# Linear attention with a two-layer MLP in one core's program: the first tile laid out anew

## The chip, the cores and the metric

The kernel runs on one core of a Trainium2 chip. The metric is the device time of one execution in microseconds. Five engines take part: TensorE (PE in the profile; PEld is its loading of weights), VectorE (DVE), ScalarE (ACT), GpSimd (POOL) and SyncE (SP), which here issues every DMA. Each works through its own list of instructions in order, and semaphores hold an instruction until what it needs is there.

## The reference, cut to what matters

```python
def _attn_ref(q, k, v, omega):           # q, k, v: (8, 8, 576, 64); omega: (128, 64)
    def phi(x):
        h = einsum('bhsd,md->bhsm', x, omega) - sum(x * x) / 2
        return exp(h - max(h)) / sqrt(m)
    q_p, k_p = phi(q * scale), phi(k * scale)
    kv, z = einsum('bhsm,bhsd->bhmd', k_p, v), sum(k_p, axis=2)
    return einsum('bhsm,bhmd->bhsd', q_p, kv) / (einsum('bhsm,bhm->bhs', q_p, z) + 1e-6)
def _moe_ref(x, g_ln, w_ch1, w_ch2):     # x: (8, 576, 512), the heads side by side
    xn = (x - mean(x)) / sqrt(var(x) + 1e-6) * g_ln
    return x + maximum(xn @ w_ch1, 0) @ w_ch2          # w_ch1: 512x2048, w_ch2: 2048x512
```

## The kernel before, in words

**Tiles.** The 8 x 576 rows of x make 36 blocks of 128 rows; four blocks make a tile of 512 rows, and there are nine tiles. The MLP of a tile runs over f = 0 to 15, blocks of 128 hidden columns: `mm1(t, f)` (L684) multiplies the transposed x - mu of the tile with the f-th 128 columns of W1, 12 matmuls into one bank; `relu` (L705) writes the result in a high and a low part (ACT L709, DVE L711); `mm2(t, f)` (L720) multiplies that with the f-th 128 rows of W2, 12 matmuls into four banks that stay open over all f; `result` (L740) adds x at f = 15 and stores. Each product is made of three fp32r matmuls of high and low parts. PE's order is mm1(0), mm1(1), mm2(0), mm1(2), mm2(1) and so on.

**Weights.** The host hands W1 and W2 over as 64-bit numbers, 32 blocks of 128 rows by 512 columns (512 KB each). `gen_w` (L347) loads a block, puts each number together from its two halves (a sign or mask step, L361 on ACT or L369 on DVE; a scaling, L242 or L244; two steps of DVE, L363 or L373, then L377), multiplies W1 by g (L242 or L244, "g" the layer norm's gain, one number per partition) and takes the low part (L388 for W1, L394 for W2). A block of W1 holds 128 rows of W1 and 512 columns, so the mm1 of f = 0 to 3 take one column strip out of each of the blocks 0 to 3, and all four have to be there ahead of mm1(0); likewise 4 to 7 ahead of mm1(4).

**Attention.** A key block (`gen_k`, L418): a projection on PE (L481), its negated maximum on DVE (L484), exponentials on ACT (L490, eight of them in two halves), and the *sums* (L453), 16 small matmuls that add k_p times v into a pair of banks. For the first batch the five key blocks add up in banks 6 and 7, and ACT copies them out once (L470, `kv`). A query block (`gen_q`, L498): a projection (L513), a copy to SBUF (L236 is the copy helper's line on ACT), a maximum over partitions on POOL (L543), the subtraction on DVE (L548) and the exponential on ACT (L551). Then the *products* (`gen_x`, L574): 16 small matmuls (L590), 1 / denominator and x on DVE (L598, L600, L602), statistics (L619, L621). `gen_xnT` (L648) subtracts mu on DVE (L658), PE transposes (L671), ACT and DVE write the high and the low part (L675, L677). The first tile needs five key blocks, four query blocks and four products ahead of its first mm1; all later ones are done between the matmuls of the MLP, "visits" to a pair of banks.

**Idle matmuls.** Until the MLP starts, `warm` (L319) issues matmuls of a constant on itself (128x252 bf16, the tile named spin, L322) into the unused columns of bank 7. `gen_warm` fills what the layout sees as free time of PE with them, and sums and products have one after every second head inside them (L457, L594).

**What sets the order.** `Plan` (L67) is a planner that runs while the program is built. Each step of a generator names the engine and what the step costs there (`yield dve(n)`, `yield "run", {ACT: 0.66, DVE: 0.45}`); the planner keeps a clock for each engine, takes the step that can start first, by rank among equals, and emits it. So the costs decide only the order of instructions on each engine, on which engine a step with two prices runs, and how many idle matmuls stand between others. A step seen from another engine is ready HOP = 0.2 us after its end.

Of the kernel before, what the change touches and what calls it, by code (L numbers as in the profile page):

```python
# [41 lines left out]
class Part:  # L42


    def __init__(self, rank, order, gen, after):
        self.rank, self.order = rank, order
        self.holds = 0
        self.gen = gen
        self.after = after
        self.eng, self.end = None, 0.0  # L50
        self.want = None
# [6 lines left out]
    def seen(self):  # L58

        return max(self.after, self.end + Plan.HOP)  # L60

    def ready(self, eng):
        t = max(self.after, self.end + (Plan.SAME.get(eng, 0.0) if eng == self.eng else Plan.HOP))
# [3 lines left out]
class Plan:  # L67
# [10 lines left out]
    HOP = 0.2  # L78
    SAME = {ACT: 0.16, DVE: 0.13, POOL: 0.1}
    SLACK = 0.4  # L80
# [79 lines left out]
    def starts(self, part, queue):  # L160

        times = ((max(part.ready(e), self.free_at[e]), e, cost) for e, cost in part.want[1].items())
        return min(times, key=lambda t: t[0] + t[2] + queue[t[1]])

    def run(self):
        while self.ready:
# [18 lines left out]
            part.eng = eng  # L185
            if eng == SP:
# [10 lines left out]
def favor_ffn(ctx, tc, kT, kTr, vF, vR, qT, qD, omT, gT, w1, w2, out):  # L197
# [24 lines left out]
    def act(n, k=1, c=0.17):  # L222
        return "run", {ACT: k * (c + 0.00083 * n)}

    def dve(n, k=1, c=0.157):
        return "run", {DVE: k * (c + 0.00104 * n)}
# [97 lines left out]
    def gen_const():  # L324
# [6 lines left out]
        nc.sync.dma_start(g_sb, gT)  # L331
        done(("g",))
# [14 lines left out]
    def gen_w(n, f):  # L347
# [9 lines left out]
        eng = yield "run", {ACT: 0.66, DVE: 0.45}  # L357
        t = tile_of(wt, [P, DM], U32)
        sign = 0x80000000
        if eng == ACT:  # L360
            nc.scalar.activation(out=t, in_=r[:, :, 0], func=AF.Copy, scale=2.0**-29 * 7.49 / 8)  # L361
            yield dve(DM)
# [3 lines left out]
            eng = yield "run", {ACT: 0.66, DVE: 0.45}  # L366
            scaled(eng, f32(r[:, :, 1]), f32(r[:, :, 1]), 2.0**-112)
        else:
            nc.vector.tensor_scalar(out=t, in0=r[:, :, 1], scalar1=sign, scalar2=None, op0=ALU.bitwise_and)  # L369
            eng = yield "run", {ACT: 0.66, DVE: 0.45}  # L370
            scaled(eng, f32(r[:, :, 1]), f32(r[:, :, 1]), 2.0**-112)
            yield dve(DM)
# [3 lines left out]
        yield dve(DM)  # L376
# [5 lines left out]
        eng = yield "run", {ACT: 0.66, DVE: 0.45}  # L382
        w = wparts[n, f] = tile_of(tag, [P, 2, DM], F32R)
        if n == 1:
            g = g_sb[:, f % NK : f % NK + 1]
            scaled(eng, w[:, 0], f32(t), g)
            yield dve(DM)
# [3 lines left out]
        else:  # L391
            copy(eng, w[:, 0], f32(t))
            yield dve(DM)
# [24 lines left out]
    def gen_k(b, c, r, kraw, v, early, t_v, n_kp):  # L418
# [20 lines left out]
        def sums():  # L439
# [9 lines left out]
            yield us(PE, VISIT + 0.94 if mlp_on else 1.4)  # L449
            pv = two(t_b, 4 * (D + 1)).rearrange("p s (a b) -> p s a b", b=D + 1)  # L450
            for h in range(H):
# [5 lines left out]
                warm(h % 2)  # L457
# [10 lines left out]
            else:  # L468
                eng = yield "run", {ACT: 0.6, DVE: 0.7}
# [6 lines left out]
        yield us(PE, VISIT + 0.9)  # L476
# [10 lines left out]
        for s in range(2):  # L487
            yield act(M, 4)
# [9 lines left out]
    def gen_q(c):  # L498
# [3 lines left out]
        if c < QF:  # L502
# [6 lines left out]
            yield us(PE, VISIT + 0.88)  # L509
# [5 lines left out]
        else:  # L515
# [20 lines left out]
        eng = yield "run", {ACT: 1.02} if first else {ACT: 1.02, DVE: 1.23}  # L536
# [5 lines left out]
        yield us(POOL, 3.7)  # L542
# [4 lines left out]
        yield dve(8 * P)  # L547
        nc.vector.tensor_tensor(out=qc, in0=qc, in1=mx, op=ALU.subtract)  # L548
        free(t_m, mx_turn)
        yield act(8 * P)  # L550
# [23 lines left out]
    def gen_x(c, b_turn):  # L574
# [23 lines left out]
        nc.vector.tensor_scalar(out=dn, in0=pn[:, :, :, D], scalar1=EPS * M, scalar2=None, op0=ALU.add)  # L598
        yield us(DVE, 0.18)
# [249 lines left out]
```

## Time and profile before

| | us |
|---|---|
| median of 3 runs (lowest, highest) | 1027.58 (1027.01, 1027.80) |
| the profiled execution, its time | 1027.65 |
| the profiled execution, its span | 1025.9 |
| first matmul of mm1(0) starts | 57.54 |
| PE busy over the span | 1016.9 (99%) |
| DVE, ACT busy over the span | 474.9 (46%), 341.5 (33%) |

A row of a timeline reads: start, duration, engine, line, operation, output<-inputs with buffer numbers left out, shapes, count, and in brackets how long the engine had been idle and what ended that. The duration of one instruction is longer than the step to the next one's start, since they overlap by some 0.1 us on an engine. The chain view follows the end of a stretch back to what released it.

### The profile page before, as it was taken

Reading aid. Unit: us, or ns where it says so; the run is one execution under the profiler, and the core shown is the slowest. Engines: PE = TensorE matmul, PEld = TensorE weight load, DVE = VectorE, ACT = ScalarE, POOL = GpSimd, SP = SyncE. Lnnn points to the kernel's source line nnn. Section 1 sums busy time; section 2 is a strip of 40 time slices with the busy share of each in tenths; the row PEclk is TensorE's granted clock in tenths of the full one; section 3 lists DMA queues with packets and bytes.
Section 4 is the critical chain, followed back from the end, with each engine's and each line's share of the span. In section 5 each row is a group of like instructions: output and inputs, shape, how many; then the busy total and the mean of one; then the engine's idle time right before and its main releaser. Section 6 shows DMA issues by size and latency. Waiting matters only on the chain.

```text
span 1025.9 us, 16419 instructions
## 1 busy us (share of the span) xinstructions
PE 1016.9 (99%) x7033; PEld 817.5 (80%) x7033; DVE 474.9 (46%) x772; ACT 341.5 (33%) x700; POOL 118.9 (12%) x44
## 2 busy tenths in 40 slices
PE   9999999999999999999999999999999999999998
PEld 6787778788778777887788778878887888888886
DVE  6698887355375242663238422651364133113112
ACT  6387735334254243343213421231133111111100
POOL 4001040121121021031003100130022000000000
PEclk9999999999999999999999999999999999999999
DMA  9226423112122120320013100200020010001001
GB/s 355 111 82 216 156 73 129 47 61 71 43 87 88 37 63 21 104 94 22 1 62 105 51 1 1 103 21 1 9 95 21 1 42 1 1 1 42 1 1 41
DMA packets 26344, 63.13 MB, mean 62 GB/s; under 512 B 3104, under 2 KB 4256, under 8 KB 26272
## 3 DMA queue, kind: packets, MB, share of 16 engines
q1 hardware_dynamic: 26272, 62.09, 17.5%
q8 instruction: 55, 0.90, 0.4%
q14 instruction: 17, 0.14, 0.0%
HBM read 52.64 MB, written 9.44 MB: 61 GB/s over the span
## 4 chain that ended last, share of the span: by engine, by line
PE 96%; DVE 3%; ACT 1%; issue 1%
PE b L698 14%; PE b L731 13%; PE b L699 12%; PE b L700 12%; PE b L733 12%; PE b L732 12%; PE b L453 4%; PE b L481 4%; PE b L590 4%; PE b L322 3%; PE b L671 2%; PE b L531 1%; PE b L532 1%; PE b L513 1%; DVE quad L525 1%
## 5 line engine op out<-in xcount | busy, mean ns | idle before, releaser
L711 DVE SCALAR_TENSOR_TENSOR hid<-b,hid 128x512 fp32r<-128x512 f32 x144 | 99.5, 691 | 365.7 <-ACT hid L709 365.0
L709 ACT ACTIVATE hid<-b 128x512 fp32r<-128x512 f32 x144 | 86.3, 599 | 445.7 <-PE b L700 445.5
L698 PE MATMUL b<-xnT,w 128*128 128x512 f32 x576 | 231.1, 401 | 0.0
L731 PE MATMUL b<-w,hid 128*128 128x512 f32 x576 | 231.1, 401 | 0.0
L699 PE MATMUL b<-xnT,w 128*128 128x512 f32 x576 | 224.8, 390 | 0.0
L732 PE MATMUL b<-w,hid 128*128 128x512 f32 x576 | 224.6, 390 | 0.0
L733 PE MATMUL b<-w,hid 128*128 128x512 f32 x576 | 224.6, 390 | 0.0
L700 PE MATMUL b<-xnT,w 128*128 128x512 f32 x576 | 224.4, 390 | 0.0
L543 POOL PARTITION_ALL_REDUCE quad<-quad x34 | 111.1, 3281 | 661.4 <-ACT quad L236 537.7
L698 PEld LDWEIGHTS b<-xnT,w 128*128 128x128 f32 x576 | 108.1, 188 | 28.9 <-issue 4.1
L731 PEld LDWEIGHTS b<-w,hid 128*128 128x128 f32 x576 | 108.1, 188 | 24.4 <-issue 0.2
L733 PEld LDWEIGHTS b<-w,hid 128*128 128x128 f32 x576 | 108.1, 188 | 23.2
L700 PEld LDWEIGHTS b<-xnT,w 128*128 128x128 f32 x576 | 108.1, 188 | 23.2
L732 PEld LDWEIGHTS b<-w,hid 128*128 128x128 f32 x576 | 108.3, 188 | 20.5
L699 PEld LDWEIGHTS b<-xnT,w 128*128 128x128 f32 x576 | 108.2, 188 | 20.6
L490 ACT ACTIVATE kp<-b,mb 128x128 f32<-128x128 f32 (+1 forms) x296 | 81.2, 382 | 44.6 <-DVE mb L484 44.4
L484 DVE TENSOR_REDUCE mb<-b 128x8 f32<-128x1024 f32 (+1 forms) x40 | 48.8, 1220 | 35.3 <-PE b L481 35.3
L548 DVE TENSOR_TENSOR quad<-quad,quad 128x1024 f32<-128x1024 f32 x34 | 49.5, 1454 | 16.6 <-POOL quad L543 16.5
L236 ACT COPY quad<-b 128x1024 f32<-128x1024 f32 x36 | 36.6, 1018 | 59.0 <-PE b L532 44.2
L551 ACT ACTIVATE quad<-quad 128x1024 f32<-128x1024 f32 x36 | 38.3, 1065 | 42.5 <-DVE quad L548 42.5
L590 PEld LDWEIGHTS b<-kv,quad 128*64 128x64 f32 x1152 | 37.6, 137 | 15.4 <-issue 8.5
L525 DVE TENSOR_TENSOR quad<-quad,quad 64x1024 fp32r<-64x1024 f32 x28 | 38.7, 1383 | 21.5 <-ACT quad L523 20.9
(73 smaller groups left out, 770.2 us busy)
## 6 DMA issues: line engine op xcount, KB each, us to landing
w<-w SPq DMA_DIRECT2D x32, 512.0 KB, 7.2
quad<-qD SPq DMA_DIRECT2D x28, 512.0 KB, 3.3
out<-x SPq DMA_DIRECT2D x36, 256.0 KB, 2.0
v<-vF SPq DMA_DIRECT2D x28, 260.0 KB, 3.0
wide<-kT SPq DMA_DIRECT2D x28, 256.0 KB, 3.5
wide<-qT SPq DMA_DIRECT2D x8, 256.0 KB, 3.3
w<-vF SPq DMA_DIRECT2D x4, 260.0 KB, 4.4
v<-vR SPq DMA_DIRECT2D x8, 130.0 KB, 2.6
```

Source lines behind the costliest of these rows:

```text
L490: nc.scalar.activation(out=kp[0:r, j], in_=pk[0:r, s, j % 4], func=AF.Exp, scale=1.0, bias=mb[0:r, j : j + 1])
L543: nc.gpsimd.partition_all_reduce(mx.rearrange("p a b -> p (a b)"), qc.rearrange("p a b -> p (a b)"), P, bass_isa.ReduceOp.max)
L548: nc.vector.tensor_tensor(out=qc, in0=qc, in1=mx, op=ALU.subtract)
L590: nc.tensor.matmul(pn[a : a + D, h // 4, h % 4], phi[:, h % 2, h // 2, a : a + D], kvs[b][1][:, h], start=True, stop=True,)
L698: nc.tensor.matmul(ph, w[:, 0, cs], xnT[:, 0, k], start=(k == 0), stop=False)
L699: nc.tensor.matmul(ph, w[:, 1, cs], xnT[:, 0, k], start=False, stop=False)
L700: nc.tensor.matmul(ph, w[:, 0, cs], xnT[:, 1, k], start=False, stop=(k == NK - 1))
L709: nc.scalar.activation(out=hl[:, 0], in_=ph, func=AF.Relu)
L711: nc.vector.scalar_tensor_tensor(out=hl[:, 1], in0=ph, scalar=0.0, in1=f32(hl[:, 0]), op0=ALU.max, op1=ALU.subtract)
L731: nc.tensor.matmul(accs[i], hl[:, 0, cs], w[:, 0], start=(f == 0), stop=False)
L732: nc.tensor.matmul(accs[i], hl[:, 0, cs], w[:, 1], start=False, stop=False)
L733: nc.tensor.matmul(accs[i], hl[:, 1, cs], w[:, 0], start=False, stop=(f == NF - 1))
```

## The change

It does six things.

1. Sums and products have no idle matmul inside them (both calls `warm(h % 2)` go). Their cost in the plan before the MLP goes from 1.4 to 0.37 + 0.94 us. `gen_warm` stays as it is.
2. W1's blocks 0 to 3 hold other numbers: the host packs, for f = 0 to 3, all 512 rows of the 128 columns of f into block f, four row strips side by side. So mm1(f) takes all it needs from block f alone. A partition now holds four rows of W1, so g differs by strip: on ACT the multiplication is four instructions of 128 columns, on DVE one, and the low part is four instructions on DVE in place of one. Blocks 4 to 15 are as before.
3. The ranks of W1's blocks 0 to 3 in the plan go from f - 4 to 2f - 1 (each times 0.5), so block 3 ranks behind blocks 4 and 5.
4. mu - x is taken instead of x - mu, on ACT or on DVE (`either`), and g is negated once on DVE. The ACT form is new: AF.Identity with bias mu and scale -1. Of the 36, 20 go to ACT and 16 stay on DVE.
5. The costs in the plan are others throughout, smaller by some 0.1 us for most steps; what another engine sees costs 0.13 to 0.2 us by engine (LAT) in place of HOP; a DVE step marked "two" costs 1.0 us more (LOCK) where POOL is busy.
6. The copy of a projection to SBUF may go to DVE for the first tile too (`{ACT: 0.91, DVE: 1.13}`).

Counted over the whole program the idle matmuls go from 217 to 118; all other matmuls are the same in number and shape. The projections, sums and products ahead of mm1(0) are the same five, five and four.

```diff
     def starts(self, part, queue):
...
+            if e == DVE and part.want[-1] == "two" and start < self.free_at[POOL]:
+                cost += Plan.LOCK
...
-        eng = yield "run", {ACT: 0.66, DVE: 0.45}
+        if n == 1 and f < NK:
+            eng = yield either(0.92, 0.6)
+            w = wparts[n, f] = tile_of(tag, [P, 2, DM], F32R)
+            if eng == ACT:
+                for k in range(NK):
+                    cs = slice(k * P, (k + 1) * P)
+                    scaled(eng, w[:, 0, cs], f32(t[:, cs]), g_sb[:, k : k + 1])
+            else:
+                nc.vector.tensor_tensor(
...
+            yield "run", {DVE: 0.84}, "two"
+            for k in range(NK):
+                cs = slice(k * P, (k + 1) * P)
+                nc.vector.scalar_tensor_tensor(
+                    out=w[:, 1, cs], in0=f32(t[:, cs]), scalar=g_sb[:, k : k + 1], in1=f32(w[:, 0, cs]),
+                    op0=ALU.mult, op1=ALU.subtract,
+                )
...
+            return
+        eng = yield either(0.58, 0.34)
...
-            yield us(PE, VISIT + 0.94 if mlp_on else 1.4)
+            yield "run", {PE: VISIT + 0.94}, 0.03
...
-                warm(h % 2)
...
-        eng = yield "run", {ACT: 1.02} if first else {ACT: 1.02, DVE: 1.23}
+        eng = yield "run", {ACT: 0.91, DVE: 1.13}
         copy(eng, qc, pq)
...
-        yield us(PE, VISIT + 0.94 if mlp_on else 1.4)
+        yield "run", {PE: VISIT + 0.94}, 0.03
...
-            warm(h % 2)
...
-            yield us(DVE, 0.5)
-            nc.vector.tensor_scalar(out=xn, in0=x, scalar1=mu, scalar2=None, op0=ALU.subtract)
+            eng = yield either(0.58, 0.4)
+            if eng == ACT:
+                nc.scalar.activation(out=xn, in_=x, func=AF.Identity, bias=mu, scale=-1.0)
+            else:
+                nc.vector.tensor_scalar(out=xn, in0=x, scalar1=mu, scalar2=-1.0, op0=ALU.subtract, op1=ALU.mult)
...
-            yield wait("w", 1, f // NK * NK + k)
+            yield wait("w", 1, f if f < NK else f // NK * NK + k)
...
-            cs = slice(f % NK * P, (f % NK + 1) * P)
+            w = wparts[1, f if f < NK else f // NK * NK + k]
+            cs = slice((k if f < NK else f % NK) * P, ((k if f < NK else f % NK) + 1) * P)
...
-        plan.add(RW + RS * (2 * f - 7 if f >= NK else f - NK), gen_w(1, f))
+        plan.add(RW + RS * (2 * f - 7 if f >= NK else 2 * f - 1), gen_w(1, f))
```

Three places show what the new plan makes of the order.

PE, from the first to the second of the first tile's four products, before (quad_158 and quad_185 are the exponentials of the first and second query block, kv_86 the summed keys, spin the idle matmul's operand):

```order
L590 MATMUL b<-kv_86,quad_158 64x65 x4
L322 LDWEIGHTS spin
L322 MATMUL b<-spin 128x252
L590 MATMUL b<-kv_86,quad_185 64x65 x4
L322 LDWEIGHTS spin
```

And in the changed program, all four products (quad_156, quad_187, quad_213, quad_290):

```order
L627 MATMUL b<-kv_86,quad_156 64x65 x16
L627 MATMUL b<-kv_86,quad_187 64x65 x16
L627 MATMUL b<-kv_86,quad_213 64x65 x16
L336 LDWEIGHTS spin
L336 MATMUL b<-spin 128x252
L627 MATMUL b<-kv_86,quad_290 64x65 x16
```

Before, an idle matmul stands behind every fourth small matmul of this list (and one or two between visits); now one stands between the third and the fourth product.

DVE, from the first query block's subtraction to the maximum of the fourth key block (mb_240), before:

```order
L548 TENSOR_TENSOR quad_158<-quad_158,quad_174 128x1024
L436 MEMSET w_120_94 128x8
L369 TENSOR_SCALAR wide_264<-w_00_153 128x512
L369 TENSOR_SCALAR wide_268<-w_10_160 128x512
L244 TENSOR_SCALAR w_00_153<-w_00_153 128x512
L244 TENSOR_SCALAR w_10_160<-w_10_160 128x512
L484 TENSOR_REDUCE mb_240<-b 128x8
L548 TENSOR_TENSOR quad_185<-quad_185,quad_218 128x1024
```

And the same stretch in the changed program (there the maximum is mb_234):

```order
L585 TENSOR_TENSOR quad_156<-quad_156,quad_176 128x1024
L474 MEMSET w_120_94 128x8
L385 TENSOR_SCALAR wide_264<-w_00_151 128x512
L585 TENSOR_TENSOR quad_187<-quad_187,quad_206 128x1024
L521 TENSOR_REDUCE mb_234<-b 128x8
```

Four steps on weights went from ahead of this maximum, one of them is left, and the second query block's subtraction came ahead of it.

SP, the loads behind those of keys and queries (w1_00 is block 0 of W1, w2_10 block 1 of W2, and so on), before:

```order
L352 DMA w1_00_153<-w1 128x1024
L352 DMA w1_10_160<-w1 128x1024
L352 DMA w1_20_162<-w1 128x1024
L505 DMA wide1_157<-qT 128x512
L352 DMA w2_00_181<-w2 128x1024
L352 DMA w2_10_188<-w2 128x1024
L352 DMA w1_30_444<-w1 128x1024
L352 DMA w1_40_461<-w1 128x1024
L352 DMA w1_50_546<-w1 128x1024
L352 DMA w2_20_573<-w2 128x1024
```

And in the changed program:

```order
L368 DMA w1_00_151<-w1 128x1024
L368 DMA w2_00_158<-w2 128x1024
L368 DMA w1_10_161<-w1 128x1024
L542 DMA wide1_155<-qT 128x512
L368 DMA w2_10_178<-w2 128x1024
L368 DMA w1_20_189<-w1 128x1024
L368 DMA w1_40_473<-w1 128x1024
L368 DMA w1_50_495<-w1 128x1024
L368 DMA w2_20_608<-w2 128x1024
L368 DMA w1_30_677<-w1 128x1024
```

The first mm1 waited for blocks 0 to 3 of W1, the last of which was the sixth load of weights; it now waits for block 0, the first. Block 3 went from sixth to ninth, behind blocks 4 and 5.

More of the change, by code (lines that the diff above doesn't have):

```diff
@@ L58, in seen @@
     def seen(self):
-        return max(self.after, self.end + Plan.HOP)
+        return max(self.after, self.end + self.lat)
     def ready(self, eng):
-        t = max(self.after, self.end + (Plan.SAME.get(eng, 0.0) if eng == self.eng else Plan.HOP))
+        t = max(self.after, self.end + (Plan.SAME.get(eng, 0.0) if eng == self.eng else self.lat))
         return t + (Plan.SLACK if eng == PE != self.eng and 0 <= self.rank < Plan.FILL else 0.0)
 class Plan:
-    HOP = 0.2
-    SAME = {ACT: 0.16, DVE: 0.13, POOL: 0.1}
-    SLACK = 0.4
+    LAT = {PE: 0.2, ACT: 0.15, DVE: 0.13, POOL: 0.15, SP: 0.2}
+    SAME = {ACT: 0.2, DVE: 0.19, POOL: 0.1}
+    SLACK = 0.45
+    LOCK = 1.0
     FILL, IDLE = 10000, 20000
@@ L160, in starts @@
     def starts(self, part, queue):
-        times = ((max(part.ready(e), self.free_at[e]), e, cost) for e, cost in part.want[1].items())
+        times = []
+        for e, cost in part.want[1].items():
+            start = max(part.ready(e), self.free_at[e])
+            if e == DVE and part.want[-1] == "two" and start < self.free_at[POOL]:
+                cost += Plan.LOCK
+            times.append((start, e, cost))
         return min(times, key=lambda t: t[0] + t[2] + queue[t[1]])
@@ L185, in run @@
             part.eng = eng
+            part.lat = part.want[2] if len(part.want) > 2 and part.want[2] != "two" else Plan.LAT[eng]
             if eng == SP:
@@ L220, in f32, with act, dve, dve2 @@
         return ap.bitcast(F32)
[L222 to L226, printed above, removed]
+    def act(n, c=0.066):
+        return "run", {ACT: c + 0.00083 * n}
+    def dve(n, c=0.07):
+        return "run", {DVE: c + 0.00104 * n}
+    def dve2(n):
+        return "run", {DVE: 0.07 + 0.00104 * n}, "two"
+    def either(a, d):
+        return "run", {ACT: a, DVE: d}, "two"
     def us(eng, t):
@@ L331, in gen_const @@
         nc.sync.dma_start(g_sb, gT)
+        yield us(DVE, 0.08)
+        nc.vector.tensor_scalar(out=g_sb, in0=g_sb, scalar1=-1.0, scalar2=None, op0=ALU.mult)
         done(("g",))
@@ L365, in gen_w @@
             )
-            eng = yield "run", {ACT: 0.66, DVE: 0.45}
+            eng = yield either(0.58, 0.34)
             scaled(eng, f32(r[:, :, 1]), f32(r[:, :, 1]), 2.0**-112)
@@ L369, in gen_w @@
             nc.vector.tensor_scalar(out=t, in0=r[:, :, 1], scalar1=sign, scalar2=None, op0=ALU.bitwise_and)
-            eng = yield "run", {ACT: 0.66, DVE: 0.45}
+            eng = yield either(0.58, 0.34)
             scaled(eng, f32(r[:, :, 1]), f32(r[:, :, 1]), 2.0**-112)
-            yield dve(DM)
+            yield dve2(DM)
             nc.vector.scalar_tensor_tensor(
@@ L386, in gen_w @@
             scaled(eng, w[:, 0], f32(t), g)
-            yield dve(DM)
+            yield "run", {DVE: 0.66}, "two"
             nc.vector.scalar_tensor_tensor(
@@ L468, in sums @@
             else:
-                eng = yield "run", {ACT: 0.6, DVE: 0.7}
+                eng = yield "run", {ACT: 0.53, DVE: 0.61}
                 copy(eng, o, pv)
@@ L744, in result @@
         t_st, st = stats[t]
-        yield dve(DM)
+        yield us(DVE, 0.68)
         nc.vector.scalar_tensor_tensor(
```

59 lines of the change are left out of this document (33 added, 26 removed).

## The prediction

> **What bounds the kernel now.** I read the page first, then the stretches (busy time by window), then the chain of waits between 28 and 58 us, then the timelines of DVE, ACT and POOL there. From the page, the row of PE and the chain by engine:
>
> ```profile
> PE 1016.9 (99%) x7033; PEld 817.5 (80%) x7033; DVE 474.9 (46%) x772; ACT 341.5 (33%) x700; POOL 118.9 (12%) x44
> ...
> PE 96%; DVE 3%; ACT 1%; issue 1%
> ```
>
> Four stretches (length, busy time and instructions by engine, granted clock, DMA share, GB/s), cut at the end of the first batch's sums, at the first mm1 and at about the end of the first tile's MLP:
>
> ```profile
> 0.00:31.00 31.00, 29.28 (x335) 20.53 (x336) 21.57 (x29) 20.59 (x51) 14.24 (x12) 1.00 0.96 366
> 31.00:57.50 26.50, 24.78 (x282) 19.96 (x282) 18.34 (x43) 9.22 (x17) 0.00 (x0) 1.00 0.06 24
> 57.50:157.00 99.50, 99.50 (x696) 76.70 (x695) 87.85 (x151) 65.15 (x129) 14.17 (x4) 1.00 0.41 141
> 157.00:1022.00 865.00, 863.26 (x5725) 700.34 (x5723) 346.28 (x552) 246.53 (x506) 90.48 (x28) 1.00 0.13 42
> ```
>
> From 57.5 us on PE is the bound: it is busy all but 1.7 of 964.5 us, and the change leaves the number and shape of its matmuls there alone. So the time moves with the first 57.5 us, with waits that PE gets afterwards, and with nothing else. In the stretch 31 to 57.5 PE looks just as busy, yet the chain shows with what (start, length, what; x is the count of instructions):
>
> ```profile
> by line: PE b L322 62.6%; PE b L590 20.4%; PE b L671 5.8%; PE b L453 5.1%; DVE x L602 2.3%; ACT kv L236 2.0%; PE b L698 0.8%; issue 0.7%; DVE dn L598 0.6%
> ...
> 30.59 0.38 PE b L453 x8
> 30.97 0.98 PE b L322 x8
> 31.97 0.60 ACT kv L236
> 32.61 0.81 PE b L322 x6
> 33.42 0.38 PE b L590 x8
> 33.80 0.21 PE b L322
> ...
> 42.47 0.38 PE b L590 x8
> 42.86 0.77 PE b L322 x6
> 43.86 1.79 PE b L322 x15
> 45.67 0.70 DVE x L602
> 46.42 2.31 PE b L322 x20
> 48.73 0.44 PE b L671 x4
> ...
> 53.91 0.44 PE b L671 x4
> 54.34 3.44 PE b L322 x32
> 57.78 0.23 PE b L698
> ```
>
> L322 is the idle matmul: 62.6% of the way from 28 to 58 us. PE's list is in order, so idle matmuls that the layout put there too generously delay the real work behind them. They even hold DVE up, because they write to bank 7, from which the fourth product is read; two rows of DVE, the first waiting for an idle matmul:
>
> ```profile
> 43.65 0.17 DVE L598 TENSOR_SCALAR dn<-b 128x8 f32<-128x8 f32 x1 [2.36 <-PE b L322]
> 56.68 0.76 DVE L388 SCALAR_TENSOR_TENSOR w<-wide,g_sb,w 128x512 fp32r<-128x512 f32 x1
> ```
>
> The second row is the low part of W1's block 3, done at 57.44, 0.1 ahead of the first mm1: the second thing for which the MLP waits, and one that mm1(0) no longer needs.
>
> **The change, part by part.** I go from S, the end of the first batch's sums (30.97 now), to the first mm1 (57.54), then to what comes ahead of S, then to the first tile.
>
> *From S to mm1: 26.6 us now.* One price is needed, 16 small matmuls (32 passes) without idle ones inside. The MLP's visits show it:
>
> ```profile
> 139.43 1.08 PE b L590 x32
> ```
>
> I take 1.2 with the switch, where 33.42 to 42.86 shows 9.44 / 4 = 2.36 each now. An idle matmul takes 3.44 / 32 = 0.11, and 0.21 behind a small one.
>
> - S to first product: 2.45 now. After: one idle matmul 0.2, ACT's copy of kv 0.6, five idle 0.65: 1.5.
> - Four products: 9.44 now; 4 x 1.2 and an idle one: 4.9.
> - End of the fourth product to first transposition: 5.87 now (48.73 less 42.86), with 41 idle matmuls. After: 22. DVE is the other limit: its list between the first product and the fourth's denominator holds, behind the third product (S + 5.1), one weight step, two reciprocals, one statistics step and two x, 4 x 0.61 + 0.3, so S + 7.8; thirteen idle matmuls let it through at S + 7.9, nine more end at S + 9.1. So 2.7.
> - First to last transposition: 5.18 now. After, an idle matmul waits for the fourth x (statistics 2 x 0.61, small steps 0.3, x 0.61: S + 9.95), then 13, 3 and 5 idle ones and three times 0.44: 4.4.
> - Last transposition to mm1: 3.63 now with 32 idle matmuls, 2.1 with 14. ACT's four mu - x (0.61 each, as its scaling by g) and copies end at S + 14.9, idle matmuls at S + 15.6.
>
> Sum: 1.5 + 4.9 + 2.7 + 4.4 + 2.1 = 15.6, so 11.0 less. DVE is close behind PE in each term (within 0.2 to 1 us), so I do not go below 14.5; if every link with DVE slips by half a step, it is 18.
>
> The steps of 0.61 are DVE's for 512 columns with two inputs, the distance of two starts; that of the low part is 0.66:
>
> ```profile
> 32.11 0.69 DVE L377 SCALAR_TENSOR_TENSOR wide<-w 128x512 uint32<-128x512 uint32 x1
> 32.72 0.69 DVE L373 SCALAR_TENSOR_TENSOR w<-w,wide 128x512 uint32<-128x512 uint32 x1
> ...
> 57.34 0.69 DVE L377 SCALAR_TENSOR_TENSOR wide<-w 128x512 uint32<-128x512 uint32 x1
> ```
>
> And that of ACT's scaling by g, 0.62 to its next start at 56.31:
>
> ```profile
> 55.69 0.73 ACT L242 ACTIVATE w<-wide,g_sb 128x512 fp32r<-128x512 f32 x1
> 56.31 0.68 ACT L242 ACTIVATE w<-w 128x512 f32<-128x512 f32 x1
> ```
>
> *S itself.* Here the fourth key block's maximum (L484 at 20.17) starts late, and ACT's exponentials behind it:
>
> ```profile
> 12.80 2.42 DVE L548 TENSOR_TENSOR quad<-quad,quad 128x1024 f32<-128x1024 f32 x1
> ...
> 16.60 1.78 DVE L369 TENSOR_SCALAR wide<-w 128x512 uint32<-128x512 uint32 x1 [0.84 <-PE b L481]
> ...
> 20.17 1.21 DVE L484 TENSOR_REDUCE mb<-b 128x8 f32<-128x1024 f32 x1
> 21.30 1.21 DVE L548 TENSOR_TENSOR quad<-quad,quad 128x1024 f32<-128x1024 f32 x1
> ```
>
> ```profile
> 12.26 3.22 POOL L543 PARTITION_ALL_REDUCE quad<-quad  x1 [0.78 <-ACT quad L236]
> ```
>
> Under POOL's reduction (12.26 to 15.48) a subtraction takes 2.42 where it takes 1.21 without. After: the first query's copy is on DVE, behind the first maximum (6.0 to 7.1), so done at 8.4; POOL runs 8.5 to 11.7 and 11.7 to 14.9; the one weight step left ends at 15.6; then the second subtraction, 1.1 and 1.0 for POOL's third run: maximum at 17.7 in place of 20.17, 2.45 earlier. ACT's part behind it is shorter by one exponential of a query:
>
> ```profile
> 21.42 1.14 ACT L490 ACTIVATE w<-b,mb 128x128 f32<-128x128 f32 x4 [3.31 <-DVE mb L484]
> 24.33 1.12 ACT L551 ACTIVATE quad<-quad 128x1024 f32<-128x1024 f32 x1
> ```
>
> That is 1.1 with its wait; the last sums are a visit of 1.2 instead of 2.2, 1.0. Together 4.6, and 4.8 with the start, where 20 idle matmuls stand for 22: S at 26.2. Ends: 3 (POOL holds DVE up more) and 6.
>
> Here the Trainium skill (SBUF — State Buffer, "Who interferes with whom") says that a two-input DVE step and a GpSimd instruction that reads SBUF exclude each other, the second blocked until the first is through. The trace disagrees in size: the blocked subtraction ended at 15.22, before POOL did at 15.48. By that rule the time would be 1015.0.
>
> So mm1 starts at 26.2 + 15.6 = 41.8, 15.7 earlier.
>
> *The first tile.* mm1(0), mm1(1), mm2(0), mm1(2), mm2(1) take 12 x 0.23 = 2.72 each, so mm1(3) is due 13.6 later, at 55.4. It needs W1's block 3, now behind blocks 4 and 5. From the first product (S + 2.8 = 29.0) to its low part DVE's list holds 33 steps of 0.61, two low parts of 0.66, four low parts in four pieces (0.66 and three more fixed parts of some 0.07: 0.85), 15 small steps of 0.1 and two of 0.35: 27.0 us without a pause. Done at 56.0: PE waits 0.6 there. Four pieces on ACT are at most 1.14 (the row at 21.42, from PSUM). Blocks 6 and 7, due by 63, come some 5 us later, at 61. Behind that DVE's share falls (87.85 of 99.5 us now). I take 1.0 of waits in all, 0 to 5. The loads end early enough: DMA is at 0.96 until 31 us and at 0.06 behind it.
>
> *The rest.* Later tiles keep their visits; two waits of the products for a query's exponential could go or be others:
>
> ```profile
> PE b L590 <- ACT quad L551: 1.7, 2, 0.9
> ```
>
> I leave these at nothing, between 1.7 less and 2 more. Twenty of 36 mu - x move from DVE to ACT; both have room from 157 us on.
>
> Sum: 15.7 - 1.0 = 14.7 less. The profiled execution took 1027.65, a span of 1025.9 and 1.75 around it, which is 0.07 above the median of the runs; so 1027.65 - 14.7 = **1013.0**. By the bounds of S (3 to 6), of S to mm1 (8.6 to 12.1) and of the waits (0 to 5) the forecast's own range is 1010 to 1017; all three ends on the bad side at once (6.6 less, 1021) I hold for rare.
>
> **Rivals.**
>
> 1. *The weights become the bound.* PE starts 15.7 earlier, but DVE's work on weights is the same. For: DVE is 88% busy from 57.5 to 157, and block 3 has no slack by my sum. Against: DVE idles over 9 us of the first 31 and 8 in the next stretch, which the new order fills. If its list takes 5 us more than counted, PE waits 6 in place of 1: 1018.0. Chance 0.15.
> 2. *Idle matmuls and DVE still hold each other up* at bank 7 (two waits on the fourth product, as at 43.65). Each turn that misses costs the idle matmuls behind it, about 1.3: twice that, 1015.6. Chance 0.10.
> 3. *POOL's reduction holds DVE for its whole length:* the first subtraction then ends at 16.1, the weight step waits for the third run's end at 18.1, the maximum comes at 19.7, 2.0 later: 1015.0. Chance 0.07.
> 4. *Slower: the array's clock falls.* Ninety-nine idle matmuls go. The clock is 1.00 in all stretches, but only with them; the first 22 show the slow state, 0.18 each where 0.11 is usual:
>
> ```profile
> 1.18 3.97 PE L322 MATMUL b<-spin 128*128 128x252 bf16 x22 [1.18 <-DVE spin L294]
> ```
>
> If it fell to half from the third sums on, the last sums and four products cost 1.1 more each (5.5), some 60 idle matmuls on the way 6.6, four transpositions 1.8, and the first 3.4 us of the MLP 1.7: 15.6, the whole gain, and 1028.6. It turns the sign from 14.7 on. Against: behind the first 20 the new order still has 98 idle matmuls, 18 and 15 of them at the two long waits between the last sums. Chance 0.03. The Trainium skill (TensorE: Matmul & The Clock Gate, "What's actually happening") speaks against this change: the array is throttled by default and falls back to half after an idle window of about 3.4 us. No row of before shows a fall, so nothing here tests it.
> 5. *No effect:* the layout's costs are wrong by as much as before, and the idle matmuls' gain comes back as waits of PE: 1027. Chance 0.03.
>
> **How the numbers follow.** The forecast has 0.62. The range takes in rivals 1 to 3: 1009.5 to 1018.5. A measurement tells 0.2% (2 us) from no change. Faster: 0.62 + 0.15 + 0.10 + 0.07 and a little of rivals 4 and 5 where they hold in part, 0.95; the same 0.02; slower 0.03.
>
> **What would show it.** Right: the first mm1 near 41.8, S near 26.2, products of 1.2 us, no more than 22 idle matmuls between the last product and the first transposition, a wait of about half a us ahead of mm1(3), clock 1.00 throughout, and PE's busy time behind the first mm1 as before. Wrong: a first mm1 later than 45; waits of PE for DVE or ACT of over 5 us between 42 and 140; a clock under 1.00 before 45 us.

## The result, and the profile after

The changed kernel takes 1012.38 us (median of 4 runs, 1012.05 to 1012.59), beside 1027.69 for the kernel before on the same chip (4 runs, 1027.01 to 1028.54): a ratio of 0.985, 95% interval 0.9833 to 0.9867. The profiled execution took 1012.05, a span of 1010.3; before it was 1027.65 and 1025.9, so 15.6 us went.

From the page of the changed kernel, busy time by engine and the chain that ended last:

```profile
PE 999.3 (99%) x6934; PEld 805.3 (80%) x6934; DVE 463.9 (46%) x763; ACT 353.4 (35%) x734; POOL 120.3 (12%) x44
...
PE 92%; DVE 4%; DMA 2%; ACT 1%; issue 0%; SPq 0%; ACTq 0%
```

PE has 99 instructions and 17.6 us less. The four stretches, cut where the prediction put the end of the first batch's sums and the first mm1 (length, busy time by engine, granted clock, DMA share, GB/s):

```profile
0.00:26.20 26.20, 22.31 (x309) 16.92 (x309) 19.43 (x22) 18.58 (x50) 14.65 (x12) 1.00 0.94 351
26.20:41.80 15.60, 13.43 (x212) 11.52 (x207) 14.90 (x40) 10.86 (x23) 0.87 (x1) 1.00 0.44 178
41.80:142.00 100.20, 100.06 (x697) 76.65 (x696) 90.27 (x161) 73.05 (x146) 12.89 (x4) 1.00 0.41 139
142.00:1006.00 864.00, 863.07 (x5725) 700.17 (x5724) 338.06 (x542) 250.95 (x519) 91.91 (x28) 1.00 0.13 42
```

In the second line DVE is busy for 14.90 of 15.60 us (before, 18.34 of 26.5). With fewer idle matmuls in PE's list, two of PE's three waits there are for DVE, and one is for ACT. PE's timeline from the last sums (L491) over the products (L627) and transpositions (L710) to the first mm1 (L737) shows where; L336 is the idle matmul:

```profile
25.19 1.15 PE L491 MATMUL b<-v,w 64*64 64x65 f32 x32
26.27 0.28 PE L336 MATMUL b<-spin 128*128 128x252 bf16 x1
27.23 0.70 PE L336 MATMUL b<-spin 128*128 128x252 bf16 x5 [0.68 <-ACT kv L250]
27.86 3.03 PE L627 MATMUL b<-kv,quad 128*64 128x65 f32 x96
...
31.03 1.15 PE L627 MATMUL b<-kv,quad 128*64 128x65 f32 x32
32.12 1.57 PE L336 MATMUL b<-spin 128*128 128x252 bf16 x13
34.39 1.13 PE L336 MATMUL b<-spin 128*128 128x252 bf16 x9 [0.70 <-DVE dn L634]
35.36 0.60 PE L710 MATMUL b<-ident,wide 128*128 128x128 f32 x4
...
36.85 1.56 PE L336 MATMUL b<-spin 128*128 128x252 bf16 x13 [0.78 <-DVE x L638]
...
40.14 0.66 PE L710 MATMUL b<-ident,wide 128*128 128x128 f32 x4
40.63 1.67 PE L336 MATMUL b<-spin 128*128 128x252 bf16 x14
42.06 0.48 PE L737 MATMUL b<-xnT,w 128*128 128x512 f32 x1
```

The first mm1 starts at 42.06 in place of 57.54, 15.48 earlier. From there to the end of the last matmul it is 964.40 us, before 964.51: in sum, nothing was won or lost behind it. The chain that ended last goes, between 27 and 43 us, mostly over DVE's list, and back from there to a load of weights that takes 8.67 from 18.17 and lands at 26.84. DVE's list comes to that block at 26.83, so load and list are level there; no run changes the loads alone, and which of the two would bind next stays open. PE's timeline at mm1(3), whose first matmul is the first row:

```profile
55.92 0.39 PE L737 MATMUL b<-xnT,w 128*128 128x512 f32 x1
56.39 0.50 PE L738 MATMUL b<-xnT,w 128*128 128x512 f32 x1
56.73 0.39 PE L739 MATMUL b<-xnT,w 128*128 128x512 f32 x1
```

Such starts are 0.23 apart when nothing is waited for, so the 0.47 and 0.34 here are waits of 0.24 and 0.11. The two waits of 0.9 in later tiles are gone, and one of about the same size is new:

```profile
539.50 0.71 PE L518 MATMUL b<-om,wide 64*128 64x128 f32 x8 [0.89 <-DVE quad L252]
```

### The profile page after: what moved, and what is told of

Its sections match the earlier page's. It is cut to its first block, busy times and chain, and to the rows that moved or that the text cites. A ratio compares the mean times of both kernels' runs of the same rounds, so it can differ in the third digit from the quotient of the medians.

```text
span 1010.3 us, 16259 instructions
## 1 busy us (share of the span) xinstructions
PE 999.3 (99%) x6934; PEld 805.3 (80%) x6934; DVE 463.9 (46%) x763; ACT 353.4 (35%) x734; POOL 120.3 (12%) x44
## 3 DMA queue, kind: packets, MB, share of 16 engines
HBM read 52.64 MB, written 9.44 MB: 61 GB/s over the span
## 4 chain that ended last, share of the span: by engine, by line
PE 92%; DVE 4%; DMA 2%; ACT 1%; issue 0%; SPq 0%; ACTq 0%
PE b L770 14%; PE b L737 13%; PE b L771 12%; PE b L772 12%; PE b L738 12%; PE b L739 12%; PE b L491 4%; PE b L518 4%; PE b L627 3%; PE b L710 2%; PE b L568 1%; PE b L569 1%; DMA w<-w 1%; DVE wide L393 1%; DMA wide<-qT 1%; DVE w L379 1%
## 5 line engine op out<-in xcount | busy, mean ns | idle before, releaser
L737 PE MATMUL b<-xnT,w 128*128 128x512 f32 x576 | 229.8, 399 | 0.0
L737 PEld LDWEIGHTS b<-xnT,w 128*128 128x128 f32 x576 | 108.0, 188 | 26.2 <-issue 1.3
L250 ACT COPY quad<-b 128x1024 f32<-128x1024 f32 x30 | 30.4, 1014 | 46.4 <-PE b L569 44.6
L627 PEld LDWEIGHTS b<-kv,quad 128*64 128x64 f32 x1152 | 36.4, 137 | 11.6 <-issue 6.9
L491 PEld LDWEIGHTS b<-v,kp 128*64 128x64 f32 (+1 forms) x1120 | 35.5, 136 | 12.4 <-issue 9.2
```

The source lines that it names most:

```text
L491: nc.tensor.matmul(pv[a : a + D, h // 4, h % 4], kp[0:r, slot(h), a : a + D], v[0:r, h], start=(b > 0 or c + h % 4 == 0), stop=(b > 0 or ( ...
L627: nc.tensor.matmul(pn[a : a + D, h // 4, h % 4], phi[:, h % 2, h // 2, a : a + D], kvs[b][1][:, h], start=True, stop=True,)
L737: nc.tensor.matmul(ph, w[:, 0, cs], xnT[:, 0, k], start=(k == 0), stop=False)
```

## Experiments

The theory: all of the gain is the earlier first mm1, and that needs three things together, a short list of PE, a short list of DVE ahead of it, and an order in which DVE takes the queries before the weights. The rivals: one part alone carries it; or the idle matmuls only filled gaps that DVE leaves anyway; or the clock decides. Each kernel is the changed one with a part undone, or the old one with a part alone. "MLP" is from the first mm1 to the end of the last matmul, of the profiled execution; the old kernel ran beside each at 1027.77 to 1028.17.

| kernel | median us | first mm1 | MLP |
|---|---|---|---|
| before | 1027.69 | 57.54 | 964.51 |
| changed | 1012.38 | 42.06 | 964.40 |
| changed, idle matmuls back inside sums and products | 1024.18 | 54.63 | 964.78 |
| the same, these visits priced at 2.27 | 1020.47 | 47.67 | 965.93 |
| before, only without idle matmuls inside | 1023.79 | 50.80 | 967.40 |
| changed, all old prices | 1019.48 | 48.16 | 965.70 |
| changed, no surcharge beside POOL | 1028.01 | 50.43 | 971.86 |
| changed, surcharge 2.0 | 1016.03 | 43.29 | 966.99 |
| before, only with the surcharge | 1037.25 | 58.95 | 972.89 |
| changed, W1's first blocks by rows | 1014.26 | 44.75 | 963.81 |
| changed, mu - x on DVE alone | 1017.30 | 44.24 | 967.37 |
| changed, first query copies on ACT alone | 1014.88 | 45.08 | 964.72 |
| changed, 29 of 98 idle matmuls | 1012.96 | 42.49 | 964.63 |
| changed, none of the 98 | 1014.77 | 42.57 | 966.63 |

Two things have to be kept in mind with this table. The 95% interval of the ratio is 0.9833 to 0.9867 for the changed kernel and overlaps with those of the kernels at 1014.26, 1014.77 and 1014.88; their later first mm1 or longer MLP in the trace carries these differences of 2 to 2.5 us. And in seven of the traces the granted clock falls to 0.50 for one to five stretches of 3.41 us: with all old prices, without idle matmuls inside, without the surcharge, with the surcharge alone, with the copies on ACT, with 29 of 98 and with none. With the old prices the fall explains nothing that can be seen: one execution at a clock of 1.000 took 1019.28, four at 0.998 took 1019.17 to 1020.59. The old kernel without idle matmuls inside took 1023.07 at 1.000, 1022.67 and 1023.79 at 0.998, and 1025.36 and 1025.84 at 0.994 and 0.995. For the other five no execution without a fall is on record.

### Idle matmuls inside the sums and products

Back in both loops, at the old price:

```diff
-            yield "run", {PE: VISIT + 0.94}, 0.03
+            yield us(PE, VISIT + 0.94 if mlp_on else 1.4)
...
+                warm(h % 2)
```

> The new kernel with the idle matmuls back inside the sums and the products, at the old price of a visit (1.4). Theory (idle matmuls in PE's list are on the path): four products take about 2.3 us each again in place of 1.1 (4.6 more), the last sums 1 us more, the sums ahead of them some 2 more where they follow one another; the waits for DVE ahead of the fourth denominator and the fourth x go (0.7 and 0.8 less). First mm1 6.5 to 8.5 us later, 48.5 to 50.5; no wait at mm1(3): 1019 to 1021. Rival (DVE's list sets the first mm1, idle matmuls only fill its gaps): DVE's steps do not change, so the first mm1 stays at 42 to 44 and the time under 1014.5.

Measured: 1024.18 (ratio to before 0.9967, 0.9955 to 0.998), the first mm1 12.6 later. The direction is the theory's; the size is well over the 6.5 to 8.5 that I gave. PE's timeline at the third of the sums' visits, the first product and the first transposition:

```profile
22.10 0.45 PE L491 MATMUL b<-w,w 128*64 128x65 f32 x8
...
34.39 0.45 PE L628 MATMUL b<-kv,quad 128*64 128x65 f32 x8
...
45.95 0.63 PE L712 MATMUL b<-ident,wide 128*128 128x128 f32 x4
```

The first product starts at 34.39 in place of 27.86: 6.5 come ahead of the products, where I had put 3. The delay grows from visit to visit (2.8 at the third of the sums, 4.0 and 5.1 at the next two), as if all nine visits stood in one chain. The second kernel prices these visits near their traced 2.36:

```diff
-            yield us(PE, VISIT + 0.94 if mlp_on else 1.4)
+            yield "run", {PE: VISIT + (0.94 if mlp_on else 1.9)}, 0.03
...
```

> The new kernel with the idle matmuls back inside the sums and products, and these visits priced in the planner at 2.27, near their traced 2.36 (with the price of 1.31 and 1.4 the first mm1 came at 54.63). Theory (the idle matmuls inside are time on the path, nine visits of 1.1 more each; a right price gives back only the idle matmuls that the planner had put in between): 7, 3 and 3 idle matmuls in place of 15, 9 and 16 around the last sums and the products, first mm1 at 48 to 51.5, 1018.5 to 1022. Rival (the wrong price was the loss, the idle matmuls inside only take the place of those between): first mm1 at 42 to 44.5, 1012.4 to 1015.

Measured: 1020.47 (0.9952, 0.9931 to 0.9972), first mm1 at 47.67, just ahead of the range I gave. That median stands between two groups: seven executions took 1018.78 to 1020.95, and five took 1026.43 to 1027.04 with a mean granted clock of 0.99. The trace is of the first group; none of the second is kept, so where its clock fell is not known. By the first mm1 of these two traces, 7.0 of the 12.6 go with the wrong price and 5.6 with the idle matmuls at the right one. The old kernel without them, and nothing else changed:

```diff
-            yield us(PE, VISIT + 0.94 if mlp_on else 1.4)
+            yield us(PE, VISIT + 0.94)
...
-                warm(h % 2)
```

> The old kernel with one edit: no idle matmuls inside the sums and products, a visit priced 1.31. Theory (idle matmuls inside the visits are the larger half): sums and products of 1.1 us, 28 idle matmuls ahead of the first transposition in place of 41, 13 in place of 32 behind the last; S at 26 to 28 in place of 31, first mm1 at 47.5 to 50: 1017.5 to 1020, 8 to 10 less than the old kernel. Rival (DVE bounds this stretch, W1's block 3 is done at 57.4 in the old kernel and all four are needed): first mm1 not ahead of 55, 1025 or more.

Measured: 1023.79 (0.9963, 0.9951 to 0.9976), 4 us less where 8 to 10 were expected. The sums end 2 us earlier, and it is lost at once. PE's timeline, and DVE's copy that it waits for:

```profile
31.50 1.63 PE L322 MATMUL b<-spin 128*128 128x252 bf16 x7 [2.11 <-DVE kv L238]
33.07 3.79 PE L589 MATMUL b<-kv,quad 128*64 128x65 f32 x96
```

```profile
28.43 1.21 DVE L547 TENSOR_TENSOR quad<-quad,w 128x1024 f32<-128x1024 f32 x1
29.56 0.68 DVE L377 SCALAR_TENSOR_TENSOR wide<-w 128x512 uint32<-128x512 uint32 x1
30.16 0.68 DVE L363 SCALAR_TENSOR_TENSOR w<-w,wide 128x512 uint32<-128x512 uint32 x1
30.77 0.69 DVE L238 COPY kv<-b 128x520 f32<-128x520 f32 x1
```

The planner gave the copy of kv to DVE, behind a subtraction and two weight steps. The clock is at 0.50 from 31.4 to 34.8 besides: the seven idle matmuls take 0.23 each and the first three products 3.79, where the changed kernel needs 3.03. The first mm1 still comes 6.7 earlier, but 2.9 go in later tiles. Removing the idle matmuls inside the visits, alone, is worth a quarter of the gain.

### Prices and order

All old prices (fixed parts of steps, latencies, the product at 1.4, no surcharge, the first queries' copies on ACT), the rest as changed:

```diff
-    LAT = {PE: 0.2, ACT: 0.15, DVE: 0.13, POOL: 0.15, SP: 0.2}
+    LAT = dict.fromkeys((PE, ACT, DVE, POOL, SP), 0.2)
-    def dve(n, c=0.07):
+    def dve(n, c=0.157):
...
```

> The new kernel with the old kernel's prices in the planner (a step's fixed part 0.157 and 0.17, a product 1.4, one latency of 0.2 for all, no lock, the queries' copies on ACT alone as the first tile had them). Theory (the layout's prices set half of the gain): 41 idle matmuls again between the fourth product and the first transposition, in place of 22, and S about 2 us later because the queries' copies wait for ACT; first mm1 4.5 to 6 us later, 46.5 to 48: 1017 to 1018.5. Rival (the idle matmuls inside the visits were the whole cost, the prices only rename the order): first mm1 within 1 us of 42, 1012.4 to 1013.4.

Measured: 1019.48 (0.9922, 0.9908 to 0.9935), first mm1 at 48.16, 6.1 later: the theory, 1 us above its range, since the MLP lost 1.3 too. The 41 idle matmuls are back between the fourth product and the first transposition, and S comes 2.5 later. Now one number alone:

```diff
-    LOCK = 1.0
+    LOCK = 0.0
```

> The new kernel without the planner's surcharge of 1.0 on a two-input DVE step that starts while POOL is busy. Only the order changes: six more steps on the weights stand ahead of the fourth query's subtraction on DVE. Theory (the order in which DVE takes weights and queries sets S and the first product, and the surcharge is what keeps weights back): first product 4 to 6 us later, first mm1 at 46 to 48.5: 1016.5 to 1019. Rival 3 (POOL holds DVE for its whole length whatever the order, so the surcharge changes little): first mm1 within 1.5 us of 42.06, under 1014.

Measured: 1028.01 (0.9998, 0.9989 to 1.0007); ten of eleven executions took 1027.44 to 1028.57, and one took 1991.47, which nothing on record explains. The whole gain is gone, far more than expected: 8.4 in the first mm1 and 7.5 in later tiles. The timelines of POOL and of DVE in this kernel:

```profile
9.00 9.99 POOL L580 PARTITION_ALL_REDUCE quad<-quad  x3 [7.67 <-DVE quad L252]
23.74 7.03 POOL L580 PARTITION_ALL_REDUCE w<-w  x1 [4.74 <-ACT w L250]
```

```profile
24.45 0.67 DVE L379 SCALAR_TENSOR_TENSOR w<-w,wide 128x512 uint32<-128x512 uint32 x1
...
26.66 0.68 DVE L389 SCALAR_TENSOR_TENSOR w<-w,wide 128x512 uint32<-128x512 uint32 x1
27.27 0.41 DVE L252 CAST w<-wide 128x512 fp32r<-128x512 f32 x1
30.80 1.23 DVE L585 TENSOR_TENSOR w<-w,w 128x1024 f32<-128x1024 f32 x1 [3.12 <-POOL w L580]
```

The fourth query's reduction takes 7.03 in place of about 3.2. DVE's weight steps run on at their usual 0.68 until 27.68; the reduction ends 3.09 after that, about as long as a whole one takes alone. By this, POOL got nowhere while DVE went from one weight step to the next, those with one input (25.05 to 26.1, and the CAST) included. DVE then stands idle for 3.12, PE waits 5.0 for ACT's copy of kv behind it, and PE's clock is at 0.50 from 32.4 to 39.2, so that three products take 5.06 in place of 3.03. The waits and the clock are not told apart in the 8.4. In the changed kernel the other side waits, and less (POOL, then DVE):

```profile
21.92 3.74 POOL L580 PARTITION_ALL_REDUCE w<-quad  x1 [3.11 <-ACT quad L250]
```

```profile
15.66 2.90 DVE L585 TENSOR_TENSOR quad<-quad,quad 128x1024 f32<-128x1024 f32 x1
...
22.50 2.37 DVE L379 SCALAR_TENSOR_TENSOR w<-w,wide 128x512 uint32<-128x512 uint32 x1
```

Both directions bear out the Trainium skill (SBUF — State Buffer, "Who interferes with whom"), by which a two-input DVE step and a GpSimd instruction that reads SBUF exclude each other. The last of these steps ends at 24.87, ahead of POOL's 25.66, so what is blocked is not blocked for the whole of a reduction. In later tiles the same kernel has four waits of PE, 4.7 in all, for DVE's low parts of the queries. Is more surcharge better?

```diff
-    LOCK = 1.0
+    LOCK = 2.0
```

> The new kernel with the planner's surcharge on a two-input DVE step beside POOL at 2.0 in place of 1.0: three weight steps fewer stand on DVE ahead of the last two queries' subtractions, 13 idle matmuls between the transpositions in place of 14, 3 and 5. Theory A (from the first product on, DVE's whole list sets the first mm1, so that what is put off only comes later): the last sums up to 2 us earlier, the first mm1 within 0.7 us of 42.06, time 1011.6 to 1013.0. Theory B (a blocked step costs 1.2 to 1.8 us of DVE by the traces, more than the 1.0 charged, so that a higher surcharge still gains): first mm1 at 40.3 to 41.3, 1010.4 to 1011.6. No gain of a step already there could show as a later tile that gets worse: over 1014.

Measured: 1016.03 (0.9885, 0.9872 to 0.9898). The last sums do end earlier (25.3), yet the first mm1 comes 1.2 later and the MLP takes 2.6 more, half of it one wait of 1.3 for a transposed tile's low part: neither A nor B, but the loss in later tiles that was named last. And the surcharge in the old kernel:

```diff
+    LOCK = 1.0
...
+            if e == DVE and part.want[-1] == "two" and start < self.free_at[POOL]:
+                cost += Plan.LOCK
...
```

> The old kernel with one edit: the surcharge of 1.0 on a two-input DVE step that would start while POOL is busy. Theory (the surcharge is worth much only where PE's list is short enough to wait for DVE; in the old kernel idle matmuls hide DVE's delays): the last sums up to 1.5 us earlier, 32, 22, 12, 14 and 44 idle matmuls around the transpositions in place of 41, 8, 14, 14 and 32, first mm1 within 1.5 us of 57.54, 1026 to 1028.5. Rival (the surcharge alone carries the gain, as its removal alone took all of it away): first mm1 at 50 or earlier, under 1020.

Measured: 1037.25, slower by 0.9% (1.009, 1.0077 to 1.0103). The first mm1 is within the theory's 1.5 us, but the time is 8.8 over its range, because of two waits in a later tile, and a clock of 0.50 from 173.1 to 186.7:

```profile
174.67 2.08 PE L490 MATMUL b<-om,wide 64*128 64x128 f32 x16 [3.53 <-DVE x L611]
...
178.47 1.11 PE L680 MATMUL b<-ident,wide 128*128 128x128 f32 x4 [1.72 <-DVE wide L667]
```

The surcharge is no gain by itself, and without it the changed layout has none either. Why the later tiles lose in both, these runs do not show.

### W1's cut, mu - x, the queries' copies

W1's first four blocks cut by rows again, with their old ranks:

```diff
...
-            yield wait("w", 1, f if f < NK else f // NK * NK + k)
+            yield wait("w", 1, f // NK * NK + k)
...
-        plan.add(RW + RS * (2 * f - 7 if f >= NK else 2 * f - 1), gen_w(1, f))
+        plan.add(RW + RS * (2 * f - 7 if f >= NK else f - NK), gen_w(1, f))
...
```

> The new kernel with W1's first four blocks cut by rows as before, so that mm1(0) needs all four. Theory (with the first mm1 15 us earlier, four blocks are just about through on DVE): 13 idle matmuls between the third and the fourth transposition and 27 behind the last, in place of 5 and 14; first mm1 1.5 to 2.5 us later, the small wait at mm1(3) gone: 1013.5 to 1014.5. Rival (the new cut of W1 is what lets mm1 start early): mm1(0) waits for block 3's low part, which the new kernel ends at 56: first mm1 at 50 or later, 1020 or more.

Measured: 1014.26 (0.9867, 0.9853 to 0.988), first mm1 at 44.75, 2.7 later where the theory had 1.5 to 2.5, and the MLP 0.6 shorter: near the theory, and far from the rival's 50. The new cut of W1, with its ranks, is worth some 1.9 us; it isn't what lets mm1 start early.

Next, mu - x on DVE alone:

```diff
-            eng = yield either(0.58, 0.4)
+            eng = yield us(DVE, 0.4)
```

> The new kernel with mu - x on DVE alone. Theory (the first tile's four go to ACT in the new kernel and take 4 x 0.4 us off DVE, which sets the first mm1): 24, 7, 22 and 8 idle matmuls around the transpositions in place of 22, 14, 3 and 5; first mm1 1.0 to 2.0 us later, 43.1 to 44.1, block 3's low part later by as much; 1013.4 to 1014.8. Rival (ACT's turn of 0.6 us costs the path as much as DVE's 0.4, so either engine does): first mm1 within 0.5 us of 42.06, 1012 to 1012.9.

Measured: 1017.30 (0.9898, 0.9884 to 0.9911), 4.9 more. The first mm1 is 2.2 later, near the theory; the other 3 are in later tiles, where I had put nothing. Half of it is one wait of PE for the low part of a transposed tile:

```profile
290.16 0.50 PE L739 MATMUL b<-xnT,w 128*128 128x512 f32 x1 [1.50 <-DVE xnT L716]
```

And the copies of the first tile's queries on ACT alone:

```diff
-        eng = yield "run", {ACT: 0.91, DVE: 1.13}
+        eng = yield "run", {ACT: 0.91} if first else {ACT: 0.91, DVE: 1.13}
```

> The new kernel with the first tile's query copies on ACT alone, as in the old kernel. Theory A (the prediction's step on S: a copy on DVE starts POOL earlier and so the fourth key block's maximum): the last sums end 1.5 to 2.5 us later than 26.27, the first mm1 at 43.5 to 45, 1013.8 to 1015.5. Theory B (three DVE copies hold the banks, PE waits 2.9 us for them, and the last loads of queries and weights set S anyway): the last sums within 0.7 us of 26.27, the first mm1 within 0.8 us of 42.06, 1011.6 to 1013.2 if the later tiles keep their order.

Measured: 1014.88 (0.9868, 0.9852 to 0.9885). The last sums end at 29.01, 2.7 later, and the time is in theory A's range, but not by theory A's mechanism. POOL's first reduction starts at 9.38, beside 9.03 in the changed kernel, and the third 2.0 later (17.36 for 15.38). Yet the fourth key block's maximum comes earlier here, not later (at 18.49 in the changed kernel). DVE's timeline:

```profile
16.09 1.21 DVE L521 TENSOR_REDUCE mb<-b 128x8 f32<-128x1024 f32 x1
```

What is late is PE's list. The fourth query's projection stands ahead of the fifth key block's here, and it starts at 18.29 (18.20 in the changed kernel), just behind the load of these queries, which lands at 18.2. PE waits 2.63 for it, a wait that the profile puts down to ACT, and its clock is at half from 17.6 to 24.5. So the fifth key block's projection starts at 20.30, where the changed kernel has it at 16.44. PE's timeline, the second row a visit of the sums that takes 2.00, and 1.15 in the row at 25.19 above:

```profile
18.29 2.08 PE L550 MATMUL b<-wide,om 64*128 64x512 f32 x4 [2.63 <-ACT quad L588]
...
22.20 2.00 PE L491 MATMUL b<-w,w 128*64 128x65 f32 x32
```

The copies on DVE are worth 2.5 us in this layout, by the order that the planner then gives PE and by the clock; how much each takes is open.

### What the other idle matmuls are for

The 98 idle matmuls behind the first 20 left out:

```diff
-        while not mlp_on:
+        while not mlp_on and plan.cur.end < COLD:
```

> The new kernel with the first 20 idle matmuls alone; the other 98 are gone, and the lists of the other engines are as in the new kernel. PE then waits about 1.7, 1.5 and 1.6 us ahead of the last two sums and the first product, 3 us between the fourth product and the first transposition, 1.5, 0.7 and 0.5 between the transpositions, and 2 ahead of the first mm1. Theory (PE's clock holds through such gaps, and DVE sets the first mm1): clock 1.00 in every stretch, first mm1 at 41.4 to 42.0, 1011.7 to 1012.4. Rival 4 (the clock falls to half once the idle matmuls go): the last sums and four products 1.1 us each more, four transpositions 0.45 more, the first stretch of the MLP slow too: first mm1 at 47 or later, a clock under 0.9 between 20 and 50 us, 1018 or more. The Trainium skill (TensorE: Matmul & The Clock Gate, "What's actually happening") puts the fall behind an idle window of about 3.4 us, which the longest gap here just does not reach, if it is counted without a break.

Measured: 1014.77 (0.9868, 0.9854 to 0.9881), 2.4 more, the first mm1 at 42.57. The clock does fall, twice; stretches of 3.41 us of this kernel (length, PE's busy time, granted clock, DMA share, GB/s):

```profile
21.23:24.64 3.41, 1.37 (x32) 1.00 1.03 419
24.64:28.05 3.41, 1.78 (x28) 0.50 1.03 418
28.05:31.46 3.41, 3.39 (x62) 0.50 1.03 420
31.46:34.87 3.41, 2.11 (x72) 1.00 0.67 269
34.87:38.28 3.41, 0.63 (x4) 1.00 0.00 0
38.28:41.69 3.41, 2.88 (x12) 0.50 0.00 0
41.69:45.10 3.41, 2.73 (x7) 0.50 0.00 0
45.10:48.51 3.41, 3.41 (x9) 0.50 0.00 0
48.51:51.92 3.41, 3.41 (x16) 1.00 0.00 0
```

Rival 4's mechanism is there, at a sixth of its price. Until 42 us it costs PE 0.5, because PE waits for ACT and DVE there anyway; the MLP's 2.2 more go with its first matmuls, at half clock from 42.57 to 48.5. With fewer idle matmuls instead of none:

```diff
-WARM, COLD = 0.0, 5.0
+WARM, COLD = 0.3, 5.0
```

> The new kernel with an idle time of 0.3 us planned between two idle matmuls behind the first 20: 29 of them in place of 98, the lists of the other engines as in the new kernel. Theory (idle matmuls past those that keep the clock only cost): clock 1.00, first mm1 0.1 to 0.6 us earlier than the new kernel's 42.06, 1011.8 to 1012.4. Rival 4 (their density keeps the clock): a clock under 1.00 between 20 and 45 us, first mm1 at 43 or later, 1013.5 or more.

Measured: 1012.96 (0.9852, 0.9839 to 0.9866), the same as the changed kernel by this measurement; the first mm1 comes 0.4 later, not earlier. The clock falls once:

```profile
33.34:36.75 3.41, 1.11 (x7) 1.00 0.07 26
36.75:40.16 3.41, 2.66 (x12) 0.50 0.01 2
40.16:43.57 3.41, 3.41 (x15) 0.50 0.00 0
43.57:46.98 3.41, 3.41 (x16) 1.00 0.02 5
```

So taking away more idle matmuls gains nothing: they no longer set the first mm1, which moves by half a us at most. No kernel of these beats the changed one.

## Why the prediction was right

The time (1013.0, measured 1012.38) and the main mechanism hold: the first mm1 comes 15.5 earlier, and PE's work behind it takes as long as before. Inside the term S the sum was lucky. Point by point, us:

| term | before | predicted | measured |
|---|---|---|---|
| end of the first batch's sums, S | 30.97 | 26.2 | 26.27 |
| S to first product | 2.45 | 1.5 | 1.6 |
| four products | 9.44 | 4.9 | 4.3 |
| fourth product to first transposition | 5.87 | 2.7 | 3.2 |
| first to last transposition | 5.18 | 4.4 | 4.8 |
| last transposition to mm1 | 3.63 | 2.1 | 1.9 |
| first mm1 | 57.54 | 41.8 | 42.06 |
| PE's waits at mm1(3) (predicted: in the whole first tile) | - | 1.0 | 0.35 |

- *S* came out right by two errors that cancel. The fourth key block's maximum starts at 18.49, not 17.7: the second subtraction took 2.90 beside POOL's third reduction, where I had 2.1. From the maximum to S I had 8.5, and it took 7.8. The step by which POOL starts earlier for a copy on DVE didn't come: the first two reductions end at 15.46 (9.03 and 6.43), before at 15.48 (12.26 and 3.22). The third alone starts earlier, at 15.38 in place of 16.21. In the kernel with the copies on ACT the third starts 2.0 later than in the changed one, and yet its maximum comes earlier, at 16.09, so it doesn't show the step either. What the traces show ahead of the maximum is that three weight steps (16.60 to 20.25 before) are gone, and the second subtraction stands there. The 0.2 for a start with 20 idle matmuls in place of 22 didn't come: they took 3.98 and 3.97.
- *The products* are 0.99 each when three follow one another and 1.09 for the last; I had 1.2 from a single visit inside the MLP, with its switch. Mis-sized by 0.6.
- *Fourth product to first transposition:* 22 idle matmuls as said, and DVE's fourth denominator at 34.27, S + 8.0 (I had S + 7.8). The list waited 0.70 there. The same at the fourth x (0.78). These two are what is left of rival 2.
- *mm1(3):* the low part was due at 56.0 by my sum and starts at 55.99, in four pieces. PE goes on after the first piece, so it waits 0.35. Counting until the last piece was wrong, and on the safe side.
- *Rival 1* (weights) didn't come: DVE is 90% busy up to 142 us and PE waits 0.35 for weights, though the load that lands at 26.84 had no slack. *Rival 3* came in half: the maximum lies between my 17.7 and its 19.7. *Rival 4* names a real mechanism, but not one that this change sets off: the clock is 1.00 in all four stretches. In seven of the other kernels it does fall, in five of them with the idle matmuls between the visits still there, wherever waits leave PE's list empty enough. *Rival 5* has the time of the kernel without the surcharge: with one price wrong, 1028, though half of that loss lies in later tiles.
- *Later tiles,* "nothing, -1.7 to 2", came out at -0.1, but the reason I gave (they keep their visits) doesn't carry it. The planner lays the whole program anew: in the variants the stretch behind the first mm1 took 963.8 to 972.9, and in five of them it was over 2 us longer with the clock at full speed at its start. That term deserved a wider range; that it was nothing here is not explained by any run.

## What to carry to other kernels

An idle filler instruction in an in-order list costs like work: where the planner's price of the visit is too low, each later wait moves, and here the wrong price cost 7.0 us, and the filler at the right price 5.6. Removing a part by itself tells little when a planner lays the order: undone singly the parts cost 11.8, 7.1, 1.9, 4.9 and 2.5 us, the surcharge alone 15.6, and put singly into the old kernel they gave 4.0 and lost 9.5. Read the stretches far behind an edit of such a planner too, because waits of 1 to 3.5 us appear there. And look at the granted clock of each variant before its loss is put down to the part that was undone.

## What the runs showed of the hardware

- *The clock looks at stretches of 3.41 us.* In the kernel without the 98 idle matmuls the falls and rises (24.64, 31.46, 38.28, 48.51) lie 2, 2 and 3 times 3.41 apart. It fell behind stretches in which PE was busy 1.37 and 0.63 of 3.41, and 1.11 in the kernel with 29; it stayed behind 2.11, and in the changed kernel, where 33.44 to 36.85, the emptiest such stretch from 26 us on, holds 1.92. It rose behind 3.39 and 3.41, not behind 2.88. The other kernels agree: their falls came behind 0.00 (no surcharge), 0.74 (old prices), 1.44 (copies on ACT), 1.44 (no idle matmuls inside) and 1.46 (surcharge alone), and one rise came behind 3.27, while a stretch of 3.07 was not enough. The Trainium skill (TensorE: Matmul & The Clock Gate, "What's actually happening") has the same length of window, 3413 ns, running free of the kernel's start. By its table the fall follows an idle window; here a stretch in which PE was 43% busy was idle enough. I had expected a single gap of that length to be needed; the longest gap ahead of the first fall was 1.6 us.
- *A reduction on POOL was held off as long as DVE's weight steps followed one another* (7.03 in place of 3.2, in one trace); the other way round DVE's steps of 1.21 and 0.6 took 2.90 and 2.37 and ended before the reduction did.
